# Interleaving two batches' stages on TensorE, with a prologue in another order, in a linear-attention and FFT-gate kernel

## The chip, the cores and the metric

The kernel runs on one core of a Trainium2 chip, as one program and one launch. The metric is the device time of that core in microseconds (us); the change is judged by the median of several runs beside the kernel before on the same chip. The engines are named as in the profile: PE (TensorE's matmuls), PEld (its weight loads), DVE (VectorE), ACT (ScalarE), POOL (GpSimd) and SP (SyncE).

## What is computed

```python
def _attn_ref(q, k, v):                      # (8, 8, 576, 64) each
    theta = np.pi / 2.0 * np.arange(S) / S
    phi = lambda x: concat([relu(x) * cos(theta), relu(x) * sin(theta)], -1)
    q_p, k_p = phi(q), phi(k)
    kv = einsum('bhsf,bhsd->bhfd', k_p, v);  z = sum(k_p, axis=2)
    return einsum('bhsf,bhfd->bhsd', q_p, kv) / (einsum('bhsf,bhf->bhs', q_p, z)[..., None] + 1e-06)

def _moe_ref(x, w_proj, filter_fft, w_out):  # x: (8, 576, 512), the heads side by side
    x1, x2, x3 = split(x @ w_proj, 3, axis=-1)
    x2_conv = irfft(rfft(x2, axis=1) * rfft(filter_fft, axis=0), axis=1)
    return (x1 * x2_conv * x3) @ w_out
```

## The kernel before

Eight batches run through one chain of stages, each a function that issues the work of all engines for one batch b (lines of the kernel before):

- `emit_input_dma` (L100): loads of q and k by one DMA each into `raw` tiles (three buffers) and of v by six DMAs straight into `va`, one for each row residue j; all on POOL's queue, cast from fp32 to fp16 on the way.
- `emit_phi` (L360): 12 DVE operations for q (tile `qp`) and 12 for k (`kp`), each relu times a cosine or sine column, 96x512.
- `emit_qt` (L384), once per pair of heads: 12 PE transposes into a PSUM unit `qt`, then a DVE and an ACT copy into `qpt`.
- `emit_kv` (L371): 48 PE matmuls, then an ACT copy to `kvs`.
- `emit_num` (L404), once per pair of heads: 10 matmuls into `num`, and on DVE a sum, a reciprocal and the product `att` (L421).
- `emit_fx` (L428): for each of four channel groups c, 4 matmuls into `fx` and one into the shared unit `fxc`; ACT copies `fx` (L444), DVE copies `fxc` (L448).
- `emit_x2` (L458): 24 matmuls 128x512 in three blocks (L466); ACT scales each into `x2f` (L471).
- `emit_dft` (L473): 6 matmuls in three blocks (L480), an ACT copy `xf` each (L482), and four DVE products each (L485 to L490) that end in `yf`.
- `emit_gate` (L492), four times: 16 matmuls (L503) into two units; ACT copies one to `x1s` (L509), DVE makes `g` of both (L511, twice).
- `emit_inv` (L520), four times: 6 matmuls (L529), an ACT copy `eo`, three DVE operations that end in `y` (L536).
- `emit_out` (L540): 20 matmuls (L548) in three groups, ACT scales them into `os` (L552), and 9 DMAs on SP's queue store them.

All PSUM tiles are one tag of four units (L61, two banks each): a stage that opens a unit waits until the unit opened four before it has been read by ACT or DVE. Engines run their rows in order. The framework's scheduling sets each engine's row order; it keeps near the order in which the program text issues the work, but hoists rows that it holds ready. Before the loop stand the loads of batches 0 and 1 and of the weights, phi of batch 0, and the tables: `emit_cols`, `emit_fm`, `emit_rows`, `emit_fwd_tables`, and within the loop, at b = 0, `emit_inv_tables` and `emit_h` (the filter's transform: 42 matmuls into `h_ps` and `h_nyq`, L342 and L352). `trig` (L203) makes a sine and a cosine table with four DVE operations and two ACT operations.

The loop (L577) runs b from -1: x2 of b; qt and kv of n = b + 1; dft and gate of b; num of n; phi of n + 1; inv of b; fx of n; out of b.

Of the kernel before, what the change touches and what calls it, by code (L numbers as in the profile page):

```python
# [17 lines left out]
def kernel(  # L18
# [23 lines left out]
    NT = 5  # L42
# [13 lines left out]
    setupp = ctx.enter_context(tc.tile_pool(name="setupp", bufs=1))  # L56
    work = ctx.enter_context(tc.tile_pool(name="work", bufs=1))
    psum = ctx.enter_context(tc.tile_pool(name="psum", bufs=4, space=bass.MemoryType.PSUM))

# [3 lines left out]
    perm = consts.tile([NP, NP], FP16, tag="perm", name="perm")  # L63
    ccol = consts.tile([128, NJ], FP32, tag="ccol", name="ccol")
    scol = consts.tile([128, NJ], FP32, tag="scol", name="scol")
    half_pi = consts.tile([128, 1], FP32, tag="half_pi", name="half_pi")
# [10 lines left out]
    filt16 = setupp.tile([NP, NJ, DM], FP16, tag="filt16", name="filt16")  # L77
    va_buf = [consts.tile([NP, NH, NJ, 66], FP16, tag=f"va{i}", name=f"va{i}") for i in range(2)]
    qpt_buf = [consts.tile([128, NH, NT, 2, 64], FP16, tag=f"qpt{i}", name=f"qpt{i}") for i in range(1)]
# [19 lines left out]

    def emit_input_dma(b):  # L100
        for nm, src in (("q", q), ("k", k)):
            rw = work.tile([NP, NH, NJ * D], FP16, tag="raw", bufs=3, name=f"{nm}raw{b}")
            raw_t[(b, nm)] = rw
            nc.gpsimd.dma_start(out=rw, in_=src[b].rearrange("h (p j) d -> p h (j d)", j=NJ))
        va = va_buf[b % 2]
        vv = v[b].rearrange("h (p j) d -> p h j d", j=NJ)
        for j in range(NJ):
            nc.gpsimd.dma_start(out=va[:, :, j, 0:D], in_=vv[:, :, j])  # L108

    def emit_weight_dma():  # L110
        nc.gpsimd.dma_start(out=wp16, in_=moe_w_proj.rearrange("(i p) n -> p i n", p=128))
        nc.gpsimd.dma_start(
            out=filt16, in_=moe_filter_fft.rearrange("(p j) n -> p (j n)", j=NJ)
        )
        nc.gpsimd.dma_start(out=wo16, in_=moe_w_out.rearrange("(i p) n -> p i n", p=128))


    def emit_cols():
        pi_ = setupp.tile([128, 1], I32, tag="p_i", name="p_i")
        p = cc["p"] = small("p")  # L120
        nc.gpsimd.iota(pi_, pattern=[[1, 1]], base=0, channel_multiplier=1)
        nc.vector.tensor_copy(out=p, in_=pi_)
# [25 lines left out]
    def emit_fm():  # L148
# [14 lines left out]
        orow_i = setupp.tile([128, 10], I32, tag="orow_i", name="orow_i")  # L163
        nc.gpsimd.iota(orow_i, pattern=[[1, 10]], base=0, channel_multiplier=0)
# [18 lines left out]
        irow_i = setupp.tile([128, 6], I32, tag="irow_i", name="irow_i")  # L183
        nc.gpsimd.iota(irow_i, pattern=[[1, 6]], base=0, channel_multiplier=0)
# [18 lines left out]
    def trig(nr, turns, sin_dst, cos_dst, ncol):  # L203

        a = setupp.tile([NP, NCOL], FP32, tag="tg_a", bufs=2, name="tg_a")
        nc.vector.tensor_scalar(
            out=a[0:nr, 0:ncol], in0=turns, scalar1=RC, scalar2=None, op0=AL.add
        )
        nc.vector.scalar_tensor_tensor(
            out=a[0:nr, 0:ncol], in0=a[0:nr, 0:ncol], scalar=-RC, in1=turns,  # L210
            op0=AL.add, op1=AL.subtract,
        )
        nc.scalar.activation(out=sin_dst, in_=a[0:nr, 0:ncol], func=AF.Sin, scale=TWO_PI)
        b_ = setupp.tile([NP, NCOL], FP32, tag="tg_a", bufs=2, name="tg_b")
        tsc(b_[0:nr, 0:ncol], turns, 0.25, AL.add, RC, AL.add)
        nc.vector.scalar_tensor_tensor(
            out=b_[0:nr, 0:ncol], in0=b_[0:nr, 0:ncol], scalar=-RC, in1=turns,
            op0=AL.add, op1=AL.subtract,
        )
        nc.scalar.activation(  # L220
            out=cos_dst, in_=b_[0:nr, 0:ncol], func=AF.Sin, scale=-TWO_PI, bias=half_pi[0:nr]
        )

    def emit_rows():

        fr_i = setupp.tile([NP, 3, NP], I32, tag="fr_i", name="fr_i")
        nc.gpsimd.iota(fr_i[:, 0], pattern=[[3, NP]], base=0, channel_multiplier=0)
        nc.gpsimd.iota(fr_i[:, 1], pattern=[[6, 48], [4, 2]], base=1, channel_multiplier=0)
        nc.gpsimd.iota(fr_i[:, 2], pattern=[[6, 48], [2, 2]], base=2, channel_multiplier=0)
        frow = cc["frow"] = setupp.tile([NP, 3, NP], FP32, tag="frow", name="frow")  # L230
        nc.vector.tensor_copy(out=frow, in_=fr_i)
        sg_i = setupp.tile([NP, NP], I32, tag="sg_i", name="sg_i")
        nc.gpsimd.iota(sg_i, pattern=[[0, 48], [-2, 2]], base=1, channel_multiplier=0)
# [18 lines left out]
    def emit_fwd_tables():  # L252
# [15 lines left out]
        tn = setupp.tile([NP, 3, NP], FP32, tag="tn", name="tn")  # L268
# [25 lines left out]

    def emit_inv_tables():
        fc = cc["fc"]
        sr_i = setupp.tile([NP, HS], I32, tag="sr_i", name="sr_i")
        nc.gpsimd.iota(sr_i, pattern=[[2, 3], [12, NP]], base=1, channel_multiplier=0)
        srow = setupp.tile([NP, HS], FP32, tag="srow", name="srow")
        nc.vector.tensor_copy(out=srow, in_=sr_i)  # L300
# [336 lines left out]
```

## Time and profile before

| | us |
|---|---|
| three timed runs | 327.4, 327.4, 330.59 |
| median | 327.4 |
| the profiled execution's own time | 330.73 |
| its span, from the first to the last instruction | 328.9 |
| PE busy in it | 268.2 (82%) |
| DVE busy | 226.7 (69%) |
| ACT busy | 170.4 (52%) |
| POOL busy | 55.2 (17%) |

The profiled execution took about as long as the slowest of the three timed runs. Its mean granted TensorE clock is 0.962. Times in a view count from the span's start. A row of the timeline or of the chain gives start, duration, engine, line, output and inputs, and a number of instructions; a bracket holds the idle time of the engine just before, and who ended it. A matmul's shown duration has a tail that overlaps the next one, so the cost of a run of matmuls is read from start to start.

### The profile page before, as it was taken

How to read it: one execution, taken by the hardware profiler on the slowest of the kernel's cores; microseconds unless marked ns; L12 is line 12 of the kernel's file. 1: busy time of each engine (PE TensorE's matmuls, PEld its weight loads, DVE VectorE, ACT ScalarE, POOL GpSimd, SP SyncE). 2: the span in 40 equal slices, each digit the busy share in tenths (PEclk: the TensorE clock that was granted, in tenths of full speed). 3: DMA queues.
4: the chain of work that ended last, by engine and by line, in shares of the span. 5: the costliest groups of instructions: out<-in, count | busy, mean ns of one | idle time of the engine just before them, and what ended most of it. 6: DMA issues, size and time to landing. Idle time of an engine off the chain costs nothing.

```text
span 328.9 us, 6111 instructions
## 1 busy us (share of the span) xinstructions
PE 268.2 (82%) x2394; PEld 181.5 (55%) x2394; DVE 226.7 (69%) x702; ACT 170.4 (52%) x228; POOL 55.2 (17%) x80
## 2 busy tenths in 40 slices
PE   0532459699899978997899889987999889989991
PEld 0432226247657755586548654865487647765750
DVE  1963995966943997099918991899279923990770
ACT  1030327537386626682758275737483558475642
POOL 8524700520000600051004200320000000000000
PEclk9999999769999978999999999999999799999997
DMA  7999992946004965469186907590220013004004
GB/s 111 186 211 198 186 123 34 74 59 87 1 18 129 96 50 72 131 54 107 12 173 67 111 5 158 81 120 3 73 73 2 0 47 98 2 1 128 18 0 144
DMA packets 57132, 26.67 MB, mean 81 GB/s; under 512 B 39088, under 2 KB 51888, under 8 KB 57104
## 3 DMA queue, kind: packets, MB, share of 16 engines
q0 software_dynamic: 51344, 16.85, 47.4%
q1 hardware_dynamic: 5760, 9.44, 10.1%
q8 instruction: 18, 0.29, 0.3%
q14 instruction: 10, 0.08, 0.1%
HBM read 33.69 MB, written 9.44 MB: 131 GB/s over the span
## 4 chain that ended last, share of the span: by engine, by line
PE 56%; DVE 25%; DMA 8%; ACT 6%; issue 2%; POOL 1%; ACTq 0%; DVEq 0%; POOLq 0%
PE x L503 14%; PE x L466 14%; PE out L548 8%; DMA qraw<-in_q_dram 6%; PE inv L529 5%; PE qt L389 4%; DVE att L421 4%; PE h_ps L342 4%; DVE g L511 3%; DVE kp L88 3%; ACT fx L444 3%; DMA kraw<-in_k_dram 2%; PE kv L376 2%; PE dft L480 2%; DVE qp L88 2%
## 5 line engine op out<-in xcount | busy, mean ns | idle before, releaser
L503 PE MATMUL x<-fx,wp 128*128 128x288 f16 x512 | 64.4, 286 | 0.0
L503 PEld LDWEIGHTS <-wp 128*128 128x128 f16 x512 | 50.0, 98 | 14.4 <-issue 0.2
L395 DVE COPY qpt<-qt 128x600 f16<-128x600 f16 x32 | 14.9, 468 | 56.7 <-PE qt L389 56.0
L108 POOL DMA_DIRECT2D va<-in_v_dram x48 | 37.3, 782 | 97.6 <-PE kv L376 88.8
L466 PE MATMUL x<-wp,fx 128*96 128x512 f16 x192 | 46.4, 397 | 3.9 <-DVE fx L448 3.9
L548 PE MATMUL out<-wo,y 128*128 128x512 f16 x160 | 38.4, 379 | 7.2 <-DVE y L536 3.6
L466 PEld LDWEIGHTS <-fx 128*96 128x96 f16 x192 | 24.3, 129 | 24.7 <-DVE fx L448 5.8
L533 ACT CAST eo<-inv 128x576 f16<-128x576 f32 x32 | 20.4, 638 | 33.5 <-PE inv L529 32.2
L444 ACT CAST fx<-fx 128x960 f16<-128x960 f32 x32 | 28.7, 980 | 14.2 <-PE fx L436 14.2
L471 ACT ACTIVATE x2f<-x 96x1024 f16<-96x1024 f32 x24 | 24.4, 1018 | 19.8 <-PE x L466 19.8
L509 ACT CAST x1s<-x 128x576 f16<-128x576 f32 x32 | 20.4, 639 | 25.8 <-DVE g L511 19.8
L552 ACT ACTIVATE os<-out 128x1024 f32<-128x1024 f32 (+1 forms) x24 | 20.3, 880 | 23.2 <-PE out L548 22.8
L389 PE MATMUL qt<-perm,qp 96*128 96x96 f16 x384 | 20.5, 215 | 12.1 <-DVE qp L88 11.5
L548 PEld LDWEIGHTS <-y 128*128 128x128 f16 x160 | 15.0, 97 | 27.6 <-DVE y L536 9.2
L436 PE MATMUL fx<-fm,att 128*128 128x240 f16 x128 | 19.2, 286 | 11.3 <-DVE att L421 9.1
L529 PEld LDWEIGHTS <-yf 96*128 96x128 f16 x192 | 19.7, 107 | 13.7 <-DVE att L421 5.8
L389 PEld LDWEIGHTS <-qp 96*128 96x128 f16 x384 | 18.8, 102 | 14.7 <-DVE qp L88 12.6
L511 DVE TENSOR_TENSOR g<-x,x1s 128x288 f16<-128x288 f32 x64 | 26.6, 445 | 0.0
L485 DVE TENSOR_TENSOR m<-xf,ha 96x1024 f16<-96x1024 f16 x24 | 16.3, 678 | 14.4 <-ACT xf L482 14.4
L482 ACT CAST xf<-dft 96x1024 f16<-96x1024 f32 x24 | 23.4, 1013 | 4.7 <-DVE m L486 4.7
L88 DVE TENSOR_SCALAR qp<-qraw,ccol 96x512 f16<-96x512 f16 x48 | 19.3, 403 | 8.3 <-DMA qraw<-in_q_dram 8.3
L421 DVE TENSOR_TENSOR att<-num,rcp 128x640 f16<-128x640 f32 x32 | 25.0, 817 | 0.0
(152 smaller groups left out, 390.5 us busy)
## 6 DMA issues: line engine op xcount, KB each, us to landing
qraw<-in_q_dram POOLq DMA_DIRECT2D x8, 576.0 KB, 6.0
kraw<-in_k_dram POOLq DMA_DIRECT2D x8, 576.0 KB, 7.4
va<-in_v_dram POOLq DMA_DIRECT2D x48, 96.0 KB, 7.0
out_dram<-os SPq DMA_DIRECT2D x24, 192.0 KB, 2.5
out_dram<-os SPq DMA_DIRECT2D x24, 128.0 KB, 2.3
wp<-in_moe_w_proj_dram POOLq DMA_DIRECT2D x1, 1536.0 KB, 13.9
out_dram<-os SPq DMA_DIRECT2D x24, 64.0 KB, 2.0
filt<-in_moe_filter_fft_dram POOLq DMA_DIRECT2D x1, 576.0 KB, 14.1
```

The source lines that it names most:

```text
L88: nc.vector.tensor_scalar(out=out, in0=in0, scalar1=s1, scalar2=s2, op0=op0, op1=op1)
L108: nc.gpsimd.dma_start(out=va[:, :, j, 0:D], in_=vv[:, :, j])
L389: nc.tensor.transpose(u[:, hh, ds(j * NP, NP)], qp[:, j, 2 * hp + hh].rearrange("p a b -> p (a b)"), perm,)
L421: nc.vector.tensor_tensor(out=att[:, :, ds(hp * 128, 128)].rearrange("p t (h d) -> p h t d", h=2), in0=nv[:, :, :, 0:D], in1=rcp.unsqueeze ...
L444: nc.scalar.copy(out=fx[:, c, :, 0:40].rearrange("p g (u o) -> p u g o", u=2), in_=u[:, :, 0:480].rearrange("p u (g o) -> p u g o", o=20),)
L466: nc.tensor.matmul(u[0:NP, comp], fx[:, c, ds(comp * 6 + 2 * bl, 2)].rearrange("p a b -> p (a b)"), wp16[:, c, ds(DM, DM)], start=(c == 0) ...
L471: nc.scalar.mul(out=x2f[:, bl], in_=u[0:NP], mul=X2SC)
L482: nc.scalar.copy(out=xf, in_=u[0:NP])
L503: nc.tensor.matmul(u[:, hf, 0:HS], wp16[:, i, ds(w * DM + c * 128, 128)], fx[:, i, ds(12 + 6 * hf, 6)].rearrange("p a b -> p (a b)"), star ...
L511: nc.vector.tensor_tensor(out=(g[:, c, 0:HS] if hf == 0 else g[:, c, HS:S][:, ::-1]).rearrange("p (j i o) -> p j i o", j=3, i=6), in0=us[1 ...
L529: nc.tensor.matmul(u[:, comp, 0:HS], yf[:, bl, comp, ds(c * 128, 128)], tab[:, bl], start=(bl == 0), stop=(bl == 2),)
L548: nc.tensor.matmul(u[:, x], y[:, c, ds(OT[t], 128)], wo16[:, c], start=(c == 0), stop=(c == NC - 1),)
```

## The change

- Loop: it now runs b from 0 to 8. num of batch n = b + 1 stands between the blocks of x2 of b; fx of n stands group by group between the gates of b; out of batch b - 1 (not b) stands in three groups between the four qt of b + 2, followed by kv of b + 2. Phi of b + 2 stands between inv and those. `emit_out` of b comes one turn later, so `y` of two batches is alive.
- `emit_fx` makes the `fxc` unit behind the four `fx` units, and its copy goes from DVE to ACT.
- v is loaded by one DMA into a fourth `raw` buffer, in the shape of q and k, and a new ACT copy, `emit_va`, 96x3072 fp16, spreads it into `va`.
- Prologue: POOL loads q of batch 0, makes all iota tiles, then loads k, v, the filter, w_proj in three parts, and later batch 1 and w_out. Batch 0 goes through num, fx and x2 before the tables; the H tables, H and the inverse tables follow; then phi, qt and kv of batch 1.
- `trig`: the cosine's argument is the absolute value of the sine's, made on ACT, in place of two DVE operations. For the inverse tables the first two operations run on POOL.
- Buffers: `qp` and `att` two in place of one; the pool of the setup tiles is closed before the loop, and `g`, `eo`, `y` and `os` lie in a pool opened there.

```diff
     def emit_input_dma(b):
-        for nm, src in (("q", q), ("k", k)):
-            rw = work.tile([NP, NH, NJ * D], FP16, tag="raw", bufs=3, name=f"{nm}raw{b}")
...
-        for j in range(NJ):
-            nc.gpsimd.dma_start(out=va[:, :, j, 0:D], in_=vv[:, :, j])
+        load_qk(b, "q")
+        load_qk(b, "k")
+        load_v(b)
+    def load_v(b):
+        rw = work.tile([NP, NH, NJ * D], FP16, tag="raw", bufs=4, name=f"vraw{b}")
+        raw_t[(b, "v")] = rw
+        nc.gpsimd.dma_start(out=rw, in_=v[b].rearrange("h (p j) d -> p h (j d)", j=NJ))
+    def emit_va(b):
+        nc.scalar.copy(out=va_buf[b % 2][:, :, :, 0:D],
+            in_=raw_t[(b, "v")].rearrange("p h (j d) -> p h j d", j=NJ))
+    def load_wp(w):
+        nc.gpsimd.dma_start(out=wp16[:, :, ds(w * DM, DM)],
+            in_=moe_w_proj.rearrange("(i p) n -> p i n", p=128)[:, :, ds(w * DM, DM)])
...
     def trig(...):
         nc.scalar.activation(out=sin_dst, in_=a, func=AF.Sin, scale=TWO_PI)
-        tsc(b_[0:nr, 0:ncol], turns, 0.25, AL.add, RC, AL.add)
-        nc.vector.scalar_tensor_tensor(
-            out=b_[0:nr, 0:ncol], in0=b_[0:nr, 0:ncol], scalar=-RC, in1=turns, ...)
+        nc.scalar.activation(out=a, in_=a, func=AF.Abs)
         nc.scalar.activation(
-            out=cos_dst, in_=b_[0:nr, 0:ncol], func=AF.Sin, scale=-TWO_PI, bias=half_pi[0:nr])
+            out=cos_dst, in_=a, func=AF.Sin, scale=-TWO_PI, bias=half_pi[0:nr])
...
-    emit_input_dma(0)
-    emit_cols()
-    emit_weight_dma()
-    emit_pads()
-    emit_phi(0, "q")
-    emit_phi(0, "k")
-    emit_fm()
-    emit_input_dma(1)
-    emit_rows()
-    emit_fwd_tables()
+    load_qk(0, "q")
+    emit_iotas()
+    load_qk(0, "k")
+    load_v(0)
+    load_filter()
+    load_wp(1); load_wp(0); load_wp(2)
+    emit_cols()
+    emit_pads()
+    emit_phi(0, "q")
+    for hp in range(4): emit_qt(0, hp)
+    emit_phi(0, "k")
+    emit_va(0)
+    emit_kv(0)
+    emit_fm()
+    for hp in range(4): emit_num(0, hp)
+    emit_fx(0)
+    emit_x2(0)
+    emit_rows()
+    emit_fwd_tables()
+    emit_input_dma(1)
+    load_wo()
+    emit_h_tables()
+    emit_h()
+    emit_inv_tables()
+    emit_phi(1, "q")
+    for hp in range(4): emit_qt(1, hp)
+    emit_phi(1, "k")
+    emit_va(1)
+    emit_kv(1)
-    for b in range(-1, B):
+    for b in range(0, B + 1):
...
+        if 0 < b < B: emit_x2(b, (0,))
+        if nx: emit_num(n, 0); emit_num(n, 1)
+        if 0 < b < B: emit_x2(b, (1,))
+        if nx: emit_num(n, 2); emit_num(n, 3)
+        if 0 < b < B: emit_x2(b, (2,))
+        if b < B: emit_dft(b)
+        for c in range(NC):
+            if b < B: emit_gate(b, c)
+            if nx: emit_fx(n, (c,))
+        if b < B:
+            for c in range(NC): emit_inv(b, c)
+        if n + 1 < B:
+            emit_input_dma(n + 1)
+            emit_phi(n + 1, "q"); emit_phi(n + 1, "k")
+            emit_va(n + 1)
+        for x in range(4):
+            if b >= 1 and x < 3: emit_out(b - 1, (OG[x],))
+            if n + 1 < B: emit_qt(n + 1, x)
+        if n + 1 < B: emit_kv(n + 1)
```

How rows move on three engines. In the names, a number behind `x`, `num` or `dft` is the piece or the batch and piece, and the last number counts tiles. First DVE in the prologue before, behind the last copy of batch 0's transposes (qraw_196 is q of batch 1, kraw_198 its k, num_378 and num_393 are batch 0's):

```order
L395 COPY qpt_84<-qt_3_311 128x10x60
L88 TENSOR_SCALAR qp_448<-qraw_196,ccol 96x8x64
...
L88 TENSOR_SCALAR qp_448<-qraw_196,scol 96x8x64
L86 TENSOR_SCALAR rcp_0_389<-num_0_378 128x10
L88 TENSOR_SCALAR kp_461<-kraw_198,ccol 96x8x64
L420 RECIPROCAL rcp_0_389<-rcp_0_389 128x10
L86 TENSOR_SCALAR rcp_1_404<-num_1_393 128x10
L421 TENSOR_TENSOR att_377<-num_0_378,rcp_0_389 128x2x5x64
```

And DVE at the same place in the change (qraw_486 is q of batch 1):

```order
L243 TENSOR_SCALAR tg_a<-tn_h_497 96x864
L324 CAST srow<-sr_i 96x288
L244 SCALAR_TENSOR_TENSOR tg_a<-tg_a,tn_h_497 96x864
L88 TENSOR_SCALAR rcp_0_323<-num_0_312 128x10
L88 TENSOR_SCALAR rcp_1_338<-num_1_327 128x10
L447 RECIPROCAL rcp_0_323<-rcp_0_323 128x10
L447 RECIPROCAL rcp_1_338<-rcp_1_338 128x10
L448 TENSOR_TENSOR att_311<-num_0_312,rcp_0_323 128x2x5x64
...
L90 TENSOR_SCALAR qp_598<-qraw_486,ccol 96x8x64
```

Batch 0's `att` stood behind phi of batch 1; now it stands ahead of it, behind the forward tables and the first H table.

Second PE in the change, in the turn b = 2 of the loop, the first row of each piece (num is batch 3's, x and dft are batch 2's):

```order
L498 MATMUL x_2_0_1618<-wp_79,fx_1294 96x512
...
L440 MATMUL num_0_1629<-kvs_1615,qpt_82 128x65
...
L440 MATMUL num_1_1644<-kvs_1615,qpt_82 128x65
...
L498 MATMUL x_2_1_1659<-wp_79,fx_1294 96x512
...
L440 MATMUL num_2_1669<-kvs_1615,qpt_82 128x65
...
L440 MATMUL num_3_1684<-kvs_1615,qpt_82 128x65
...
L498 MATMUL x_2_2_1699<-wp_79,fx_1294 96x512
...
L512 MATMUL dft_0_1710<-x2f_1617,tre 96x512
```

Before, in the same turn, num stood in one piece between the gates and inv (again the first row of each piece):

```order
L466 MATMUL x_2_2_1589<-wp_79,fx_1501 96x512
...
L389 MATMUL qt_0_1599<-perm,qp_1429 128x96
...
L376 MATMUL kv_1659<-va_83,kp_1442 128x65
...
L480 MATMUL dft_0_1711<-x2f_1568,tre 96x512
...
L413 MATMUL num_0_1834<-kvs_1708,qpt_84 128x65
...
L413 MATMUL num_3_1879<-kvs_1708,qpt_84 128x65
...
L529 MATMUL inv_0_1932<-ire,yf_1710 128x288
```

The pieces of num now have x2 blocks between them, and dft follows the last x2 block at once, where qt and kv stood between them before.

Third ACT in the same turn of the change (vraw_2385 is v of batch 5, the copy that `emit_va` adds):

```order
L426 COPY qpt_82<-qt_3_1551 128x2x5x60
L408 CAST kvs_1615<-kv_1566 128x520
L114 COPY va_84<-vraw_2385 96x48x64
L503 ACTIVATE x2f_1617<-x_2_0_1618 96x1024
L503 ACTIVATE x2f_1617<-x_2_1_1659 96x1024
L503 ACTIVATE x2f_1617<-x_2_2_1699 96x1024
L514 CAST xf_0_1713<-dft_0_1710 96x1024
L514 CAST xf_1_1724<-dft_1_1721 96x1024
L541 CAST x1s_0_1762<-x_2_0_1744 128x576
```

The copy of v stands between `kvs` and the first `x2f`, two turns ahead of the kv that reads it; before, no such row was there, and the three `x2f` stood ahead of the `qpt` copies and of `kvs`.

223 lines of the change are left out of this document (129 added, 94 removed).

## The prediction

> **What bounds the kernel now.** I read the page first, then the chain that ended last, then the stretch of the six equal turns.
>
> ```profile
> span 328.9 us, 6111 instructions
> ...
> PE 268.2 (82%) x2394; PEld 181.5 (55%) x2394; DVE 226.7 (69%) x702; ACT 170.4 (52%) x228; POOL 55.2 (17%) x80
> ...
> GB/s 111 186 211 198 186 123 34 74 59 87 1 18 129 96 50 72 131 54 107 12 173 67 111 5 158 81 120 3 73 73 2 0 47 98 2 1 128 18 0 144
> ```
>
> PE is busiest. Of the 40 slices of the span the first six move 111 to 211 GB/s, the loads; most later ones move less.
>
> ```profile
> 98.14 5.18 PE x L466 x24
> 103.31 2.04 PE qt L389 x48
> 105.36 1.52 PE kv L376 x48
> 106.88 1.31 PE dft L480 x6
> 108.19 7.95 PE x L503 x64
> ...
> 232.68 2.38 PE out L548 x11
> ...
> 299.25 5.19 PE x L466 x24
> ```
>
> The chain shows x2 of batch 1 starting at 98.14 and that of batch 7 at 299.25: six turns of (299.25 - 98.14) / 6 = 33.5 us. The span is so 98.1 of prologue with batch 0, 201.1 of turns, and 29.7 of last batch; 1.8 lie around it (330.73 - 328.9).
>
> ```profile
> 98.14:299.25 201.11, 184.15 (x1765) 128.20 (x1764) 144.79 (x414) 118.56 (x157) 23.84 (x31) 0.97 0.47 69
> ```
>
> In the windows view the columns behind the length are PE, PEld, DVE, ACT and POOL busy. Per turn PE is busy 30.7, DVE 24.1, ACT 19.8: no engine but PE is near 33.5. What keeps PE from less is in its own timeline of one turn:
>
> ```profile
> 185.96 0.47 PE L413 MATMUL num<-kvs,qpt 128*128 128x65 f16 x10 [0.30 <-DVE g L511]
> ...
> 189.28 0.54 PE L529 MATMUL inv<-ire,yf 96*128 96x288 f16 x3 [0.70 <-DVE att L421]
> ...
> 192.38 0.57 PE L436 MATMUL fx<-fm,att 128*128 128x240 f16 x4
> ...
> 192.87 0.57 PE L436 MATMUL fx<-fm,att 128*128 128x240 f16 x4
> ...
> 195.90 0.60 PE L548 MATMUL out<-wo,y 128*128 128x512 f16 x2 [1.12 <-DVE y L536]
> ```
>
> Between gates and inv, four nums of 0.47 each stand in 189.28 - 185.96 + 0.30 = 3.6 us, because DVE is still at g and att, and out waits 1.12 for y. These waits are what the loop's new order goes for.
>
> **The loop, part by part.** The same matmuls run. Their work per turn from these rows: x2 5.2, qt 2.0, kv 1.5, dft 1.3, gates 7.95, num 4 x 0.47 = 1.9 (tails included), fx 4 x 0.49 = 2.0 (192.87 - 192.38 with one fxc), out 20 x 0.216 = 4.3 (2.38 / 11), and inv from the last batch, where nothing stops it:
>
> ```profile
> 305.54 0.38 PE L480 MATMUL dft<-x2f,tre 96*96 96x512 f16 x1 [0.24 <-ACT x2f L471]
> ...
> 313.81 0.53 PE L529 MATMUL inv<-ire,yf 96*128 96x288 f16 x3
> ...
> 316.75 0.38 PE L548 MATMUL out<-wo,y 128*128 128x512 f16 x1
> 317.43 4.41 PE L548 MATMUL out<-wo,y 128*128 128x512 f16 x19 [0.29 <-DVE y L536]
> ```
>
> 2.9 (316.75 - 313.81). The sum is 29.1. What goes: the 3.6 around num becomes 1.9, since x2 blocks stand between; out's 1.12 and the waits beside it go, since out of b - 1 has its y since the turn before and qt fill its gaps. What comes:
> - dft right behind x2. The last batch has this order now, and its row says 0.24. I take 0.25.
> - num behind DVE. In the change 6 rows of phi q and 9 of phi k stand on DVE between the last qpt copy and the first sum of num, and att of a pair must be done before the third num (same PSUM unit) and before the third x2 block.
>
> ```profile
> 158.44 2.88 DVE kp L88 x11
> ...
> 190.48 1.46 DVE att L421 x2
> ```
> ```profile
> L395 DVE COPY qpt<-qt 128x600 f16<-128x600 f16 x32 | 14.9, 468 | 56.7 <-PE qt L389 56.0
> ```
>
> A phi row costs 2.88 / 11 = 0.26, att 0.73. From the end of the last qt, DVE needs 0.6 (the copy, 0.47, and its hand-over) + 15 x 0.26 + 1.3 (a phi row, the sum, the reciprocal, att) = 5.8 to the first att and 1.2 more to the second; PE meanwhile does kv 1.5, x2 1.7, two nums 0.9, x2 1.7 = 5.8. I count 0.2 for the third num and 0.3 for the third x2 block. Behind them wait dft and the gates.
> - the copy of v on ACT, ahead of the first x2f in every turn. No row has 3072 elements; the nearest give a slope:
>
> ```profile
> L533 ACT CAST eo<-inv 128x576 f16<-128x576 f32 x32 | 20.4, 638 | 33.5 <-PE inv L529 32.2
> L471 ACT ACTIVATE x2f<-x 96x1024 f16<-96x1024 f32 x24 | 24.4, 1018 | 19.8 <-PE x L466 19.8
> ```
>
> (1018 - 638) / 448 = 0.85 ns an element, so 2.75. From the end of kv: kvs (520 elements, 0.6 by the slope), v 2.75, x2f 1.0 = 4.4, while PE has x2, two nums and x2, 4.3, before the fourth num needs that unit. Cost 0.1; all of 1.0 if the copy took a third longer. ACT grows to 19.8 + 2.75 + 0.8 (fxc, 768 elements by the slope) = 23.4, DVE loses that cast: both stay under 29.
> - smaller pieces: each change of unit meets a hand-over; I add 0.2.
>
> A turn is then 29.1 + 0.25 + 0.5 + 0.1 + 0.2 = 30.1. Lower end 28.9 (no waits, tails hidden), upper end 33.5 (all waits come back). The value sits nearer the lower end since each wait was found with the other engines at 80% or less.
>
> One v load in place of six frees POOL and the queues, but no PE wait in the turns goes back to a load; I count nothing. If loads turned late, the ACT row of v would feel it first (third rival).
>
> Turns 1 to 5 cost 5 x 30.1 = 150.5. Turn 6 has no qt and kv: 30.1 - 3.6 = 26.5. The last batch: before 328.9 - 299.25 = 29.7. It now also has out of batch 6 (4.3) behind inv 7, which hides the 0.29; but `os` is one buffer, so its ACT copies for batch 7 wait until the stores of batch 6 have landed. The span ends 7.1 us behind the last matmul (317.43 + 4.41), copies, stores and end together, so they land between 2 and 7 us behind the last matmul of out 6. At 4 the three copies (2.5) end 1.0 later than they would, at 7 it is 4. I count 1.0: 34.7.
>
> **The prologue.** What holds it now:
>
> ```profile
> 10.42 0.35 DVE L88 TENSOR_SCALAR qp<-qraw,scol 96x512 f16<-96x512 f16 x1
> ...
> 30.27 0.35 DVE L88 TENSOR_SCALAR qp<-qraw,ccol 96x512 f16<-96x512 f16 x1 [8.35 <-DMA qraw<-in_q_dram]
> ...
> 34.28 0.82 DVE L421 TENSOR_TENSOR att<-num,rcp 128x640 f16<-128x640 f32 x1
> 45.91 8.03 PE L466 MATMUL x<-wp,fx 128*96 128x512 f16 x24 [3.27 <-DVE fx L448]
> 61.24 3.81 PE L342 MATMUL h_ps<-filt,hc 96*96 96x512 f16 x9 [3.06 <-ACT hc L220]
> ...
> 75.53 0.38 PE L480 MATMUL dft<-x2f,tre 96*96 96x512 f16 x1
> ```
> ```profile
> qraw<-in_q_dram POOLq DMA_DIRECT2D x8, 576.0 KB, 6.0
> ...
> wp<-in_moe_w_proj_dram POOLq DMA_DIRECT2D x1, 1536.0 KB, 13.9
> ```
> ```profile
> 24.89 2.36 PE L413 MATMUL num<-kvs,qpt 128*128 128x65 f16 x40 [0.68 <-ACT kvs L381]
> ```
>
> The second fence gives each load's size as it lands and the median time to landing. num of batch 0 is done at 27.2, but att waits behind phi of batch 1, whose q lands at 30.3; so x2 of batch 0 starts at 45.9, H at 61.2, dft at 75.5. In the change I follow the rows of the new order, with the same durations:
> - iotas first: the columns are ready by 5 in place of 10.4, and q of batch 0, alone in the queue, lands after about 6 us of issue at 1.3 (the page's median is 6.0). phi q starts at 7.5, phi k ends at 16.3.
> - v lands at about 12.7; ACT copies it 14.6 to 17.3 behind the qpt copies; kv ends at 20, kvs (behind the forward table's ACT rows) at 22, num at 24.
> - att, behind forward tables and the first H table on DVE, 24 to 28; fx copies on ACT behind that table's three ACT rows end at 31: x2 of batch 0 starts at 31, 15 earlier than now.
> - then ACT waits for v of batch 1. Up to it the queue moves q, k and v of two batches (6 x 0.59 MB), the filter (as large as q of a batch, 0.59) and w_proj (1.57): 5.7 MB at about 200 GB/s from 3.3 on, 32. Copy to 34.7, then three x2f with the second H table between: hc at 40.6.
> - H: 42 matmuls, 38.5 to 47.7; qt and kv of batch 1 wait for the `ha` and `hi` copies, with the copy of v of batch 2 among them (landing 45): kv ends at 52.5.
> - num of batch 1 ends at 54.7; the copy of v of batch 3 stands ahead of xf on ACT and lands near 54 (9.8 MB at 200 GB/s): xf from 57. Gates start at 58.6, inv ends at 71.4, qt and kv of batch 2 take 4.5 with DVE behind y: x2 of batch 1 at 76.
>
> So 76 in place of 98.1, with a batch's qt and kv done (3.6) and its out not yet (4.3). The ends: 70, if v copies never wait, and 88, if H runs at half clock (below, +5) and POOL's two table operations delay the loads behind them. No POOL row has their form; the nearest are these:
>
> ```profile
> L209 DVE SCALAR_TENSOR_TENSOR tg_a<-tg_a,tn_h 96x864 f32<-96x864 f32 x2 | 2.1, 1040 | 0.0
> ...
> L298 POOL IOTA sr_i<- 96x288 int32 x1 | 0.4, 400 | 0.0
> ```
>
> Three iotas of that size are 1.2, DVE's row is 1.04, so 2.2 for two operations, and I take 3.5 for what a row with inputs may cost more. They hide behind the loads; at 10 the loads of batches 2 and 3 behind them on POOL, and ACT's copies, move by 6.
>
> **The clock.** The windows view again:
>
> ```profile
> 61.80:72.04 10.24, 10.24 (x25) 4.00 (x24) 7.87 (x21) 2.24 (x3) 3.24 (x3) 0.51 0.75 51
> ...
> 119.80:126.70 6.90, 6.90 (x32) 4.55 (x33) 6.87 (x25) 2.73 (x5) 0.78 (x1) 0.52 0.01 2
> 256.30:259.80 3.50, 3.50 (x18) 2.25 (x17) 3.48 (x12) 1.51 (x3) 0.00 (x0) 0.54 0.00 0
> ```
>
> The column behind POOL is the granted clock: three stretches ran at half. In the first lay H, which took 75.5 - 61.2 = 14.3 in place of 42 x 0.216 = 9.1. It began behind a wait of 3.06 (the row at 61.24); in the change PE has no gap over 2 us from 31 on, so I take H at 9.1 and no half stretch in the turns. If H halves again, the time is 5 more; if both others come back too, half of 6.9 + 3.5 is another 5: 299.
> The Trainium skill's page "TensorE: Matmul & The Clock Gate", section "Part 1: The HAM clock gate (the "warmup" mystery)", says that the clock halves after an idle window of about 3.4 us and returns after a window of that length busy. By that rule the new order keeps its clock from H on, 289; the rule does not cover the two stretches in the turns, ahead of which no row of the timeline shows PE idle for that long, and going by them it is up to 299.
>
> **Sum.** 1.8 + 76 + 150.5 + 26.5 + 34.7 = 289.5; I forecast 289. The sum is made against the profiled 330.73, but it holds no half-clock stretch in the turns, where that execution lost some; so it stands beside the median, 327.4, which is faster by 3.3.
>
> **The rivals.**
> - The loop gains little: PE's waits return as waits for PSUM units, since four units serve more, smaller pieces. For it: every piece waits for a copy of an engine that serves two batches. Against: DVE and ACT at 24 in 30. A turn of 32.7: 289 + 5 x 2.6 + 2 = 304.
> - The prologue gains little: it becomes one of loads, because ACT and DVE stand in line for batches 1, 2 and 3. For it: 48 us of loads at the rate seen; against: they run beside H. x2 of batch 1 at 89: 302.
> - Slower: the copy of v on ACT, ahead of x2f, waits for its load in each turn, and x2f, dft and gates behind it. The load is issued when phi q of the batch before is read, some 21 us ahead of the copy; it lands 6 us later by the median. It decides from a landing over 21; to reach 327.4 each of six turns must lose 6.4, a landing of 27. The worst landing in the prologue, with all queues full, is 18.9:
>
> ```profile
> DMA to landing us min/median/max: 7.6/8.4/18.9
> ```
>
> - The change does not do what it says: the pieces run as before, hidden work moves, and prologue and loop gains are each under 2 us: 326.
> - Better: turns of 29 and x2 of batch 1 at 72: 279.
>
> **How the numbers follow.** Forecast 283 to 298 with 289 likeliest 0.70; little gain in the loop 0.12; in the prologue 0.08; better 0.03; slower 0.04; no change 0.03. The range 279 to 304 takes in the half clocks, the first two rivals and the better case, and leaves out less than 2 in 10. Faster by over 1%, about what a measurement here can tell from no change, is 0.70 + 0.12 + 0.08 + 0.03 = 0.93; within 1% 0.03; slower by more 0.04.
>
> **What would show it.** In the new profile: turns from x2 to x2 of 29 to 31; num pieces with waits under 0.5 on PE; the wait for x2f at dft near 0.25; out without a wait for y; in the prologue no DVE wait for q of batch 1 ahead of att, x2 of batch 0 at 31 and of batch 1 near 76; the v copies near 2.75. It is wrong if turns stay over 32, if ACT's v copies wait for loads in the turns, or if H's matmuls show a clock of 0.5.

## The result, and the profile after

The changed kernel takes 304.43 us (median of four runs, 303.41 to 306.0) against 329.0 (327.4 to 330.69) beside it: a ratio of 0.9257, with a 95% interval of 0.9177 to 0.9336. It is faster, as forecast, but by 25 us and not by 38, and lies 0.4 outside the range. The profiled execution, the slowest of the four, took 306.0 with a span of 304.2. From its page, in the order of the rows shown of before:

```profile
span 304.2 us, 6038 instructions
...
PE 257.1 (85%) x2394; PEld 182.1 (60%) x2394; DVE 213.3 (70%) x684; ACT 199.8 (66%) x248; POOL 38.4 (13%) x43
...
PEclk9999998558999599999999999999999999999997
...
GB/s 101 210 206 202 181 13 198 164 27 69 13 70 78 76 158 18 141 129 105 41 117 174 62 44 115 1 1 86 74 0 2 131 27 2 0 155 3 0 156 155
```

The sixth slice moves 13 GB/s, in the middle of what the prediction took for 48 us of steady loads, and the granted clock (PEclk) is at half in the eighth and ninth. PE's timeline shows the starts of x2 (L498), and the two long waits between them:

```profile
30.76 6.83 PE L498 MATMUL x<-wp,fx 128*96 128x512 f16 x24 [1.47 <-ACT fx L479]
...
56.84 3.04 PE L416 MATMUL qt<-perm,qp 96*128 96x96 f16 x36 [8.15 <-ACT hi L375]
...
87.78 1.90 PE L498 MATMUL x<-wp,fx 128*96 128x512 f16 x8
...
101.97 0.59 PE L512 MATMUL dft<-x2f,tre 96*96 96x512 f16 x1 [6.63 <-ACT x2f L503]
...
125.18 1.90 PE L498 MATMUL x<-wp,fx 128*96 128x512 f16 x8
...
129.63 0.79 PE L440 MATMUL num<-kvs,qpt 128*128 128x65 f16 x20 [0.19 <-DVE att L448]
130.69 1.93 PE L498 MATMUL x<-wp,fx 128*96 128x512 f16 x8 [0.27 <-DVE att L448]
...
133.73 0.38 PE L512 MATMUL dft<-x2f,tre 96*96 96x512 f16 x1 [0.24 <-ACT x2f L503]
...
154.81 1.90 PE L498 MATMUL x<-wp,fx 128*96 128x512 f16 x8
...
268.47 5.34 PE L498 MATMUL x<-wp,fx 128*96 128x512 f16 x24
```

| term of the sum | forecast | measured |
|---|---|---|
| prologue until x2 of batch 1 | 76 | 87.8 |
| turn 1 | 30.1 | 37.4 |
| turns 2 to 5, each | 30.1 | 29.5 (29.6, 29.6, 29.6, 29.2) |
| turn 6 | 26.5 | 25.2 |
| last batch | 34.7 | 35.7 |

A turn in which nothing is late is what was forecast: waits of 0.19, 0.27 and 0.24, and nothing else. The whole miss, 11.8 + 7.3 = 19.1, lies ahead of 125 us; what follows gave 2.6 of it back. What is late there stands on ACT and on POOL:

```profile
53.06 2.75 ACT L114 COPY va<-vraw 96x3072 f16<-96x3072 f16 x1 [5.91 <-DMA vraw<-in_v_dram]
55.72 0.59 ACT L374 ACTIVATE ha<-h_ps 96x512 f16<-96x512 f32 x1
...
98.25 2.75 ACT L114 COPY va<-vraw 96x3072 f16<-96x3072 f16 x1 [7.51 <-DMA vraw<-in_v_dram]
```
```profile
31.68 9.09 POOL L238 TENSOR_SCALAR tg_a<-tn_inv 96x864 f32<-96x864 f32 x1 [12.74 <-DVE tn_inv L90]
40.85 2.00 POOL L241 TENSOR_TENSOR tg_a<-tg_a,tn_inv 96x864 f32<-96x864 f32 x1
42.81 0.84 POOL L106 DMA_DIRECT2D kraw<-in_k_dram  x1
43.66 0.77 POOL L111 DMA_DIRECT2D vraw<-in_v_dram  x1
...
87.56 3.23 POOL L111 DMA_DIRECT2D vraw<-in_v_dram  x1 [5.63 <-DVE qp L90]
```

The copy of v of batch 2 waits until 53.06 for a load issued at 43.66; the copies of H behind it (`ha`, `hi`) free the PSUM units that the transposes of batch 1 wait for. In turn 1 the copy of v of batch 4 waits until 98.25 for the load issued at 87.56, an issue that itself took 3.23, and `x2f`, dft and the gates wait behind it. The windows view (length; PE, PEld, DVE, ACT and POOL busy, each with its number of rows; then the granted clock, the DMA share and GB/s) shows what follows the first wait:

```profile
48.70:56.80 8.10, 0.00 (x0) 0.00 (x0) 0.47 (x1) 3.74 (x4) 0.70 (x1) 0.63 1.31 203
56.80:71.80 15.00, 14.20 (x147) 10.91 (x147) 11.44 (x34) 10.26 (x13) 0.84 (x2) 0.52 0.62 83
```

PE stood still for 8.1 us and then worked 15 us at 0.52 of its clock.

### The profile page after: what moved, and what is told of

The parts are those of the page before. It is cut to its first block, busy times and chain, and to the rows that moved or that the text cites. A ratio compares the mean times of both kernels' runs of the same rounds, so it can differ in the third digit from the quotient of the medians.

```text
span 304.2 us, 6038 instructions
## 1 busy us (share of the span) xinstructions
PE 257.1 (85%) x2394; PEld 182.1 (60%) x2394; DVE 213.3 (70%) x684; ACT 199.8 (66%) x248; POOL 38.4 (13%) x43
## 4 chain that ended last, share of the span: by engine, by line
PE 59%; DVE 17%; DMA 9%; ACT 5%; POOL 3%; issue 3%; SPq 1%; ACTq 0%; POOLq 0%; DVEq 0%
PE x L535 21%; PE out L584 9%; PE inv L561 7%; DMA vraw<-in_v_dram 7%; PE x L498 6%; PE qt L416 6%; DVE kp L90 5%; PE fx L463 4%; POOL tg_a L238 3%; DVE qp L90 3%; DVE att L448 3%; PE dft L512 2%; ACT x2f L503 2%; DMA qraw<-in_q_dram 2%; PE kv L403 2%
## 5 line engine op out<-in xcount | busy, mean ns | idle before, releaser
L535 PE MATMUL x<-fx,wp 128*128 128x288 f16 x512 | 69.7, 292 | 0.0
L535 PEld LDWEIGHTS <-wp 128*128 128x128 f16 x512 | 51.1, 100 | 15.0 <-issue 1.0
L498 PE MATMUL x<-wp,fx 128*96 128x512 f16 x192 | 46.6, 391 | 2.8 <-ACT fx L479 1.5
L467 ACT CAST fx<-fx 128x960 f16<-128x960 f32 x32 | 30.3, 958 | 15.2 <-PE fx L463 15.2
L416 PE MATMUL qt<-perm,qp 96*128 96x96 f16 x384 | 23.6, 222 | 17.0 <-DVE qp L90 8.6
L584 PE MATMUL out<-wo,y 128*128 128x512 f16 x160 | 37.4, 379 | 0.0
L416 PEld LDWEIGHTS <-qp 96*128 96x128 f16 x384 | 21.1, 106 | 22.2 <-DVE qp L90 9.9
L498 PEld LDWEIGHTS <-fx 128*96 128x96 f16 x192 | 22.8, 127 | 18.9 <-DVE att L448 2.0
L114 ACT COPY va<-vraw 96x3072 f16<-96x3072 f16 x8 | 22.0, 2754 | 16.0 <-DMA vraw<-in_v_dram 16.0
L426 ACT COPY qpt<-qt 128x600 f16<-128x600 f16 x32 | 20.0, 661 | 13.9 <-DVE qpt L422 13.8
L422 DVE COPY qpt<-qt 128x600 f16<-128x600 f16 x32 | 14.7, 466 | 14.2 <-PE qt L416 13.8
L561 PEld LDWEIGHTS <-yf 96*128 96x128 f16 x192 | 18.6, 98 | 4.4
L403 PE MATMUL kv<-va,kp 96*128 96x65 f16 x384 | 15.8, 206 | 5.5 <-ACT va L114 4.0
## 6 DMA issues: line engine op xcount, KB each, us to landing
wp<-in_moe_w_proj_dram POOLq DMA_DIRECT2D x3, 512.0 KB, 14.2
```

The costliest lines, as they stand in the source:

```text
L416: nc.tensor.transpose(u[:, hh, ds(j * NP, NP)], qp[:, j, 2 * hp + hh].rearrange("p a b -> p (a b)"), perm,)
L467: nc.scalar.copy(out=fx[:, c, :, 0:40].rearrange("p g (u o) -> p u g o", u=2), in_=u[:, :, 0:480].rearrange("p u (g o) -> p u g o", o=20),)
L498: nc.tensor.matmul(u[0:NP, comp], fx[:, c, ds(comp * 6 + 2 * bl, 2)].rearrange("p a b -> p (a b)"), wp16[:, c, ds(DM, DM)], start=(c == 0) ...
L535: nc.tensor.matmul(u[:, hf, 0:HS], wp16[:, i, ds(w * DM + c * 128, 128)], fx[:, i, ds(12 + 6 * hf, 6)].rearrange("p a b -> p (a b)"), star ...
L561: nc.tensor.matmul(u[:, comp, 0:HS], yf[:, bl, comp, ds(c * 128, 128)], tab[:, bl], start=(bl == 0), stop=(bl == 2),)
L584: nc.tensor.matmul(u[:, x], y[:, c, ds(OT[t], 128)], wo16[:, c], start=(c == 0), stop=(c == NC - 1),)
```

## The experiments

**What made the loads late.** First the table operations went back to DVE (`NCOL, True)` to `NCOL)` in the call of `trig` for the inverse tables).

> The changed kernel with the first two operations of the inverse tables back on DVE. Theory A (the loads of k and v of batch 2 stand on POOL behind the table operation of 9.09 us, and the copy of v on ACT stands ahead of the copies of H that free PSUM): those loads are issued at 36 to 37 in place of 42.8 and 43.7, v lands near 46 in place of 53.0, PE's wait of 8.15 ahead of the transposes of batch 1 falls to about 2, and if that is short enough to keep the clock, about 5 us of half-clock work go too: 293. Rival B (the loads are bound by bandwidth and land when they do): v still lands near 53, 304. Rival C (load earlier, clock halves anyway): 298. All three leave the second wait, 6.63 us at the first turn.

304.33, ratio 0.926 (0.9184 to 0.9335): no gain by the medians. In the profiled execution, the fastest of its four, x2 of batch 1 starts at 85.72, 2.1 earlier. POOL's timeline, and DVE in the windows view (length, DVE busy and its rows, granted clock, DMA share, GB/s):

```profile
36.02 6.66 POOL L106 DMA_DIRECT2D kraw<-in_k_dram  x1 [17.20 <-ACT va L114]
42.67 0.77 POOL L111 DMA_DIRECT2D vraw<-in_v_dram  x1
```
```profile
36.00:42.60 6.60, 6.30 (x25) 1.00 0.23 35
```

With the table operations gone, the load of k was issued as early as theory A said, at 36.0, but the issue itself now took 6.66 us, to the end of an unbroken run of DVE rows, 25 of them in 6.6 us: phi of batches 1 and 2. Theory A named the wrong holder; nor was it B (bandwidth) that held the issue, since the DMA engines moved 35 GB/s there. The next theory, A2, was that POOL can't issue a load while DVE runs phi rows. If so, v of batch 2 must be issued ahead of them, which needs more buffers. Three edits stand in this kernel at once: two more buffers, the table operations on DVE, and two casts left out to make room:

```diff
-        ... tag="raw", bufs=4 ...
+        ... tag="raw", bufs=6 ...
...
-        sgn = cc["sgn"] = setupp.tile([NP, NP], FP32, tag="sgn", name="sgn")
-        nc.vector.tensor_copy(out=sgn, in_=sg_i)
+        sgn = cc["sgn"] = sg_i
...
-        srow = setupp.tile([NP, HS], FP32, tag="srow", name="srow")
-        nc.vector.tensor_copy(out=srow, in_=sr_i)
+        srow = sr_i
...
-        trig(NP, tn, iim..., ire..., NCOL, True)
+        trig(NP, tn, iim..., ire..., NCOL)
```

> The changed kernel with six raw buffers, the inverse tables on DVE (as in the first experiment), and the two casts of iota tiles left out so that it fits. The first experiment showed that POOL's load of k of batch 2, first in its queue at 36.0, itself took 6.66 us, as long as DVE ran phi rows. Theory A2 (POOL can issue no load while DVE runs phi rows back to back, so the loads must be issued ahead of 31): v of batch 2 now has a buffer from the start, is issued near 20, lands by 33, and PE's wait of 6 to 8 us ahead of the transposes of batch 1 falls under 2; x2 of batch 1 at 79 in place of 87.8, and the second wait is gone as with five buffers: 289. Rival B (bandwidth): v of batch 2 still lands after 45, 297 as with five buffers.

291.92, ratio 0.8866 (0.8813 to 0.8919). v of batch 2 is issued at 21.54, another load is still held (6.94), and PE's waits ahead of the transposes are small:

```profile
21.54 0.90 POOL L111 DMA_DIRECT2D vraw<-in_v_dram  x1 [1.80 <-ACT tg_a L248]
36.08 6.94 POOL L106 DMA_DIRECT2D qraw<-in_q_dram  x1 [13.65 <-ACT va L114]
```
```profile
48.23 0.67 PE L414 MATMUL qt<-perm,qp 96*128 96x96 f16 x12 [0.35 <-ACT hi L373]
...
51.27 1.18 PE L414 MATMUL qt<-perm,qp 96*128 96x96 f16 x24 [1.41 <-ACT hi L373]
53.19 2.79 PE L401 MATMUL kv<-va,kp 96*128 96x65 f16 x48 [0.74 <-ACT qpt L424]
```

A2 was right about the issue and not about the landing, which it put at 33. The chain shows the transfer from its issue on:

```profile
21.54 22.71 DMA vraw<-in_v_dram
44.27 2.75 ACT va L114
```

v of batch 2 landed at 44.3, in a queue that moved 188 to 213 GB/s in each slice of the page from the second to the sixth, up to 43.6. So with an early issue the bytes set the landing, and it is the 45 of the prediction; in the changed kernel, where the sixth slice moved 13 GB/s, it was 53.1. What the held queue cost is about this gap of 8.8, since four buffers would have let k of batch 2 be issued at 36.0 (the first experiment); rival B is right for the rest.

x2 of batch 1 starts at 81.87, 5.9 earlier than in the changed kernel and 2.9 later than A2 said; kv and what follows still ran at half clock (2.79 for kv, 1.69 in later turns). With five buffers, and nothing else changed:

> The changed kernel with five raw buffers in place of four. The load of v of batch 4 is then released by phi k of batch 2 (done at 81.0) and no longer by phi q of batch 3 (done at 87.5). Theory E (the second wait, 6.63 us ahead of dft in the first turn, is that buffer): v lands near 91 in place of 98.2, the turn falls from 37.4 to about 30, and 0.8 goes at the first wait, whose v load still stands behind the table operations: 296.5. Rival (the wait is a late transfer, whatever its issue): 304.

297.47, ratio 0.9041 (0.8984 to 0.9098). The first wait stays in the main (5.50 and 0.96), turn 1 is 29.5: theory E holds. The second wait was a buffer that came free late, not a slow transfer.

**The copy of v on ACT.** v by six loads straight into `va`, as before the change, and no copy:

```diff
-        nc.gpsimd.dma_start(out=rw, in_=v[b]...)
+        for j in range(NJ):
+            nc.gpsimd.dma_start(out=va_buf[b % 2][:, :, j, 0:D], in_=vv[:, :, j])
...
```

> The changed kernel with v loaded by six transfers straight into its place, as before the change, and without the copy on ACT; POOL keeps the table operations. Theory A (both of PE's waits, 8.15 and 6.63 us, come from the copy of v standing on ACT ahead of rows that PE needs): both go, and with them the half clock behind them, x2 of batch 1 near 76 and every turn at 29.6: 285. Rival B (bandwidth): the other loads still make batch 1 late, 300 or more. Rival D (the six transfers keep POOL's queue so long that k and q come late): one wait is replaced by another, 293 to 300.

297.58, ratio 0.9046 (0.8983 to 0.9108). The wait of 8.15 shrinks to 2.27 and 0.86, and that of turn 1 is gone, so the copy was how the late loads reached PE. But theory A's 285 is missed: a wait of 3.46 for att is new in the prologue, x2 of batch 1 starts at 82.27, and the first three turns became slower, 31.0, 30.8 and 30.8. In such a turn POOL issues six loads, 4.64 us, beside DVE's phi of k:

```profile
113.56 4.64 POOL L111 DMA_DIRECT2D va<-in_v_dram  x6 [8.88 <-PE kv L400]
```
```profile
113.90 0.54 DVE L90 TENSOR_SCALAR kp<-kraw,ccol 96x512 f16<-96x512 f16 x1
...
116.93 0.58 DVE L90 TENSOR_SCALAR kp<-kraw,ccol 96x512 f16<-96x512 f16 x1
```
```profile
118.88 0.48 PE L437 MATMUL num<-kvs,qpt 128*128 128x65 f16 x10 [1.05 <-DVE att L445]
119.93 1.93 PE L495 MATMUL x<-wp,fx 128*96 128x512 f16 x8 [0.57 <-DVE att L445]
```

Every other phi row takes 0.54 to 0.61 in place of 0.34, att comes later, and PE waits 1.62 where it waited 0.46. So the contention goes both ways, and one load in place of six is worth 1.2 us a turn.

**POOL beside DVE, by itself.** Three kernels that compute nothing of the reference, each seen in one execution.

> A kernel by itself, that computes nothing of the reference and stores zeros: POOL runs its two table operations (96x864 fp32) twice with DVE idle, then twice while DVE runs 90 phi rows (96x512 fp16) back to back, about 24 us. Theory A2: with DVE idle the first operation takes 1 to 3 us and the second 2; beside the phi rows one of them is held for many us, up to the end of the 90 rows. Rival H (the 9.09 us are POOL's own cost for this operation or for its first use): near 9 with DVE idle too, the first time or every time, and no longer beside the phi rows.

With DVE idle the two operations took 3.09 and 2.00, beside the rows 3.11 and 2.00: not held at all; it was DVE that lost. The two windows hold POOL's first operation beside the rows, and a stretch with DVE alone:

```profile
15.10:18.30 3.20, 3.12 (x8) 1.00 1.05 349
...
25.60:45.20 19.60, 19.57 (x75) 1.00 0.49 159
```

8 rows in 3.2 us, where alone it does 12. Here POOL had begun first, by 0.06; but its next three operations, begun while DVE's run was on, were not held either (2.00, 3.11 and 2.00). In the next kernel DVE had begun first.

> A kernel by itself, that computes nothing of the reference and stores zeros: four stretches of 60 DVE rows back to back; the fifth row of each releases one piece of POOL work, so that here, other than in the run before, DVE is at work first. Stretch a: phi rows and a POOL TENSOR_SCALAR of 96x512; b: phi rows and a load of 576 KB, issued by POOL; c: rows of two fp16 inputs in SBUF and the POOL operation; d: rows that read PSUM and the POOL operation. Theory A2 (a run of phi rows that began first holds POOL until it ends): in a the operation shows some 14 us (55 rows of 0.26) and its own time of about 2, in b the issue shows some 14 us in place of 0.77; c is open, in d the operation takes about 2. Rival I (something else held POOL in the prologue): about 2 and 0.8 in all four.

```profile
16.16 2.05 POOL L99 TENSOR_SCALAR oa<-lda 96x512 f32<-96x512 f16 x1 [1.87 <-DVE lda L72]
32.90 14.53 POOL L104 DMA_DIRECT2D ldb<-in_q_dram  x1 [14.69 <-DVE ph L72]
54.77 20.13 POOL L99 TENSOR_SCALAR oc<-ldc 96x512 f32<-96x512 f16 x1 [7.33 <-DVE ldc L79]
78.84 1.92 POOL L99 TENSOR_SCALAR od<-ldd 96x512 f32<-96x512 f16 x1 [3.95 <-DVE ldd L84]
```
```profile
32.52 14.51 DVE L72 TENSOR_SCALAR ph<-raw,col 96x512 f16<-96x512 f16 x55
```

The issue of a load was held for the whole run, as A2 said; the operation was held by rows with two SBUF inputs (20.13), not by rows that read PSUM (1.92), and, against A2, not by phi rows (2.05). So the last kernel gave it the shapes of the prologue, at several moments.

> A kernel by itself, that computes nothing of the reference and stores zeros: five stretches of 40 phi rows on DVE, in each of which three DVE rows of 96x288 fp32, as those that make the turns of the inverse table, release one piece of POOL work. Stretches a, b and e: the two table operations, 96x864 fp32; c: the second of them alone; d: a load of 576 KB. Theory A3 (in the changed kernel the table operation ended 3.0 us after DVE's run of phi rows in two kernels, so the run held it): in a, b and e the first operation shows what is left of the run, 10, 5 and 10 us, and its own 3.1. Rival J (a POOL operation gets in between the phi rows, as in stretch a of the run before, and something else made 9.09 of it): 3.1 in each, while the issue of the load in d is held to the end of the run, 10 us.

```profile
14.00 3.15 POOL L107 TENSOR_SCALAR oa<-srca 96x864 f32<-96x864 f32 x1 [13.56 <-DVE srca L100]
...
33.77 8.38 POOL L107 TENSOR_SCALAR ob<-srcb 96x864 f32<-96x864 f32 x1 [14.53 <-DVE srcb L100]
...
59.47 10.59 POOL L116 DMA_DIRECT2D ldd<-in_q_dram  x1 [11.86 <-DVE ph L72]
...
76.72 3.14 POOL L107 TENSOR_SCALAR oe<-srce 96x864 f32<-96x864 f32 x1 [6.67 <-DVE srce L100]
```
```profile
33.86 5.33 DVE L72 TENSOR_SCALAR ph<-raw,col 96x512 f16<-96x512 f16 x20
```

Theory A3 and rival J were each half right. In stretch b the operation was held to the end of the run (33.86 + 5.33 = 39.2) and then took 3.0, as in the changed kernel (run to 37.8, end at 40.8); in a and e the same operation got in at once. What decides is not settled: in all three DVE's row had begun first, by 0.16 or 0.17 us. A load's issue was held by each long run above (6.66, 6.94, 14.53, 10.59), while the six in a turn of the kernel with six loads of v got in between phi rows and slowed them, and in the changed kernel the issue at 8.51, beside phi q of batch 0, took 0.80. The Trainium skill's page "SBUF — State Buffer", section "Who interferes with whom", has the two engines share a port pair for which the one that starts first locks the other out for its whole instruction; in these traces a held POOL waited for a whole run of 20 to 55 rows, not for one, and who began first does not tell a, b and e apart.

**The clock.** 36 matmuls behind H, into a PSUM bank that nobody reads, in the changed kernel:

> The changed kernel with 36 more matmuls behind H that write a bank nobody reads, so that PE is busy through most of its first wait; nothing else is touched. Theory A with the clock (PE's 8.15 us of idleness are followed by half-clock work from 56.8 to 71.8): transposes, kv, num, dft and the first gate of that stretch run at 1.5, 1.5, 1.3, 1.3 and 2.0 in place of 3.0, 2.7, 2.4, 2.9 and 3.3, of which ACT and DVE give back some: 5 us less, 299.5. Rival (the half clock costs nothing there because ACT and DVE set the pace): 304.

303.58, ratio 0.9213 (0.9142 to 0.9283); the interval holds no difference and 5 us alike. The trace shows more: the stretch behind the wait ran at full clock, and x2 of batch 1 came at 84.74, 3.0 earlier. It is the fastest of its four executions beside the slowest of the changed kernel's, so part of the 3.0 may be the spread of the runs.

```profile
48.00:57.00 9.00, 8.46 (x50) 3.52 (x49) 0.29 (x1) 3.86 (x4) 0.81 (x1) 1.00 1.30 200
57.00:72.00 15.00, 11.58 (x174) 9.32 (x174) 13.70 (x40) 11.92 (x16) 0.85 (x2) 1.00 0.59 82
```

PE was busy for 11.58 us in place of 14.20. Of the 5 expected, the rest went to waits of PE for att and xf (0.91, 0.37 and 1.16), which the slow clock had covered. The same in the kernel with six buffers, with 12 matmuls:

> The kernel with six raw buffers and the inverse tables on DVE, with 12 more matmuls behind H into a bank that nobody reads, so that PE is busy through the gaps ahead of the transposes of batch 1. There, kv, num and dft of batch 1 ran at half clock (kv 2.79 in place of 1.53). Theory (the half clock costs about 3 us, as the run with 36 such matmuls showed): x2 of batch 1 at 79, 289. Rival (the gaps behind it, at the waits for qpt, kvs and att, bring the half clock all the same): 292.

290.26, ratio 0.8779 (0.8747 to 0.8812): the best time here, with x2 of batch 1 3.7 earlier:

```profile
78.16 1.90 PE L500 MATMUL x<-wp,fx 128*96 128x512 f16 x8
```

The gain over 291.92 is 1.7 by the medians, and the two intervals overlap. In the traces 1.3 of the 3.7 is lost again in the last batch, where ACT waits 5.98 in place of 4.64 for the stores that free `os`.

**The parts.** The loop's stages in their new order, but each in one piece:

> The changed kernel with its prologue, its stage order and its buffers, but each stage of the loop in one piece: x2, then the four num, dft, the four gates, then fx, inv, out of the batch before, the four transposes, kv. Theory F (the turn fell from 33.5 to 29.6 because small pieces of the other batch cover the waits for att, for the fx copies and for qpt): num waits about 1.7 again, the fx units wait about 2 for their ACT copies, the turn is 33 to 33.5: 6 x 3.6 more, 326. Rival G (what helped is that out and phi stand a turn apart; the pieces give little): turns under 30.6, 304 to 310.

307.7, ratio 0.9328 (0.9264 to 0.9392). Rival G: turns of 30.6. The small pieces are worth 1.0 of the 3.9 us that a turn gained; by subtraction the order of the stages and the one load of v (1.2, above) are worth the rest; no run takes the order alone. num in one piece behind x2 hardly waits:

```profile
122.13 5.36 PE L498 MATMUL x<-wp,fx 128*96 128x512 f16 x24
127.33 1.08 PE L440 MATMUL num<-kvs,qpt 128*128 128x65 f16 x30
128.60 0.47 PE L440 MATMUL num<-kvs,qpt 128*128 128x65 f16 x10 [0.19 <-ACT x2f L503]
```

> The changed kernel with the loop as changed and the prologue's calls in the order of before: all loads of batch 0 first, phi of q and k, the forward tables ahead of the transposes, phi of batch 1 ahead of fx of batch 0, H last. Theory (the order of the prologue is worth the 10.3 us by which x2 of batch 1 comes earlier, 87.8 against 98.1): 314, with turns of 29.6. Rival (the prologue is bound by loads and by the same ACT copies in either order): 304 to 307.

312.99, ratio 0.9499 (0.9445 to 0.9554). x2 of batch 1 starts at 102.77, later than in the kernel before, but turn 1 is then 29.5, as v has landed long before: 15.0 lost in the prologue, 7.9 won back. The net, 7.1 by the traces and 8.6 by the medians, is the worth of the new order as it stands. The 314 expected came near by luck: it had 10.3 in the prologue and nothing in turn 1.

Two small parts, `fxc` on DVE in the kernel with six buffers, and the cosine tables by DVE in the changed kernel:

> The kernel with six raw buffers and the inverse tables on DVE, with the copy of fxc back on DVE, where it was before the change. If that move was worth something, because DVE is busier than ACT, turns of 29.6 become 30 or more and the time 294 to 296; if it was worth nothing, since PE is the bound of a turn, 292.

291.69, ratio 0.8796 (0.8745 to 0.8847), turns of 29.6: worth nothing that shows.

> The changed kernel with the cosine tables made by two DVE operations again, in place of the absolute value on ACT: four tables, 1.6 us of DVE for each large one, 5 in all, ahead of phi of batch 1 and 2, less 3 us on ACT. Theory A2 (POOL is free again when the run of phi rows ends): the loads of k and v of batch 2 are issued up to 4 us later than 42.8 and 43.7, x2 of batch 1 comes 2 to 5 later: 306 to 309. Rival (DVE has room there): 304.

306.49, ratio 0.9261 (0.9213 to 0.9309), no difference that can be told. x2 of batch 0 starts 6.6 later (37.33), the load of v of batch 2 is issued 3.8 later (47.44), but PE waits 2.17 there in place of 8.15 and x2 of batch 1 starts at 87.94, as in the changed kernel: what Abs saved ahead of x2 of batch 0 was lost again in the wait for v.

## Why the prediction was right and wrong

- **Turns, 30.1: right**, 29.6, by the waits named. The reason given was only a part: it had small pieces cover num. In one piece num behind x2 lost almost as little, because DVE is then not busy with g. The forecast's number would have stood; its lever, as far as the runs tell, was mostly the order and the load.
- **v copy, 2.75: right**, 2.75 to 2.77 in every row. That ACT and DVE stay under PE in a turn was right too: from 125.18 to 243.25 PE was busy for 115.5 us, DVE for 92.5 and ACT for 89.6.
- **"One v load in place of six ... I count nothing": wrong by 1.2 a turn.** Six issues on POOL slow phi on DVE, on which num waits.
- **x2 of batch 0 at 31, hc at 40.6, H 38.5 to 47.7: right** (30.8, 41.3, 37.4 to 48.1).
- **The step that failed: "with the copy of v of batch 2 among them (landing 45)".** It came at 53.1. The landing was taken from bytes at 200 GB/s, as if POOL's queue never stood; it stood from 31.7 to 42.8 beside phi of batches 1 and 2. The bytes themselves were right: issued ahead of phi, the same load landed at 44.3. The prediction did ask what the table operations cost with POOL alone (3.5, measured 5.1) and what 10 would do, but sought the cost in the operation and not in DVE's rows beside it. Without them the next load is held all the same. kv of batch 1 ended at 62.5 in place of 52.5, so 10 of the 11.8 were lost by then. With the load early x2 of batch 1 came 5.9 earlier, and with the clock kept too (the next point) 3.7 more, at 78.16; 2.2 over the forecast stay unexplained.
- **"PE has no gap over 2 us from 31 on": fell with it.** 8.15 of wait, then half clock, worth 3.0 and 3.7 in the traces of the two kernels that kept PE busy, and 0.9 and 1.7 by their medians. H itself ran at full clock, as forecast.
- **Turn 1: the third rival in one turn.** "It decides from a landing over 21" took the steady turn, where the load is issued 20 us ahead of the copy. In turn 1 it was issued at 87.56, behind phi q of batch 3, which DVE runs late there, and the issue was held for 3.23 beside phi k: 6.63 of PE wait and some half clock, 7.3. The prediction's own sign of being wrong, v copies that wait for loads in the turns, showed here. The rival was priced as all turns or none; one turn of it was the likely case, since the first turn has the prologue's delays.
- **The range.** 88 stood as the prologue's end if POOL was late, and 304 as the rivals' price, each alone. Here the late prologue and the late turn 1 came together, 19.1. That 87.8 met the 88 is luck in part, since H, whose half clock was to make 5 of it, ran at full clock. So is it that the second rival (89 and 302) came near: it laid the time to the rate of the loads, and in the slice from 38.0 to 45.6, while they were held, the DMA engines moved 13 GB/s.

## What to carry to other kernels

A load's landing is its issue plus its transfer behind the bytes queued ahead of it, and the issue is a row on POOL's timeline that can be held like any other; follow every load of a prologue back to the row that frees its buffer and to what DVE runs while it is issued. Where a copy stands in an in-order engine ahead of rows that another engine waits for, its load must be early, or the copy stand behind them: here late loads of v, through ACT, left the prologue 11.8 us and turn 1 7.3 us over the forecast; with two buffers more and the tables on DVE the prologue was 5.9 over and turn 1 on time (291.9), and with the clock kept it was 2.2 over (290.3). Price the first turn of a steady loop by itself.

## What was not expected of the hardware

POOL and DVE hold each other up: the issue of a 576 KB load, 0.77 us by itself, took 6.66 to 7.84 in the prologue of four of the kernels and 10.59 and 14.53 beside runs of 40 and 55 phi rows. A POOL operation that gets in slows DVE, 8 rows in 3.2 us in place of 12. On POOL one input and a scalar pair (3.09) cost more than two inputs (2.00), 96x864 fp32 each. The half clock outlasted the wait that it came with: 15 us at 0.52 with PE busy for 14.2 of them; and in the kernel with six buffers it came behind waits of 1.41 at most, where PE was busy for about half of the time:

```profile
48.00:52.00 4.00, 2.07 (x42) 1.85 (x42) 1.53 (x6) 4.00 (x9) 0.84 (x2) 1.00 1.31 204
52.00:56.00 4.00, 3.25 (x59) 3.03 (x57) 2.75 (x9) 2.79 (x5) 0.00 (x0) 0.54 1.31 204
```

The rule that the prediction cites from the Trainium skill ("TensorE: Matmul & The Clock Gate", Part 1: half after an idle window of about 3.4 us, full again after a busy one) agrees with these traces in the length of its window, and not in what counts as idle or busy. In the clock record of every trace of the full kernels, each stretch at half clock that ends before the program does lasts a whole number of 3.41 us: 20.48 and 6.83 in the changed kernel, 3.41 and 13.65 with six buffers, and in the kernel with 12 more matmuls there is none from 38 us on while PE works.

But the windows of 3.41 us that ended in a halving were not all idle: PE was busy for 1.30 us in the one up to 50.8 in the changed kernel, 2.1 us into its long wait, for 0.17 in the one up to 98.6, and for 1.76 with six buffers, up to 52.4. And one busy window did not always bring the full clock back: it did at 105.4, but PE was also busy all through from 57.6 to 61.0, and the clock stayed at half until 71.3. What the chip counts as busy stays open. Ahead of the first record, at 33.7 in the changed kernel, the clock column reads 1.00, yet kv and num of batch 0 took 2.80 and 2.36 there, as in the half stretch: the rows say more than the column.
